# Moving the score mask, a softmax product and a value copy between engines in a recurrent-memory transformer kernel

## The chip, the cores and the metric

The kernel is one program on one core of a Trainium2 chip. It drives TensorE (PE, matrix products; PEld is its weight load), VectorE (DVE), ScalarE (ACT), GpSimd (POOL) and the DMA queue of SyncE (SP). The engines run side by side, each through its own list of instructions in order, and wait for each other on semaphores. The metric is the device time of one execution in microseconds (us), the median over several runs of the same program. Besides these runs one execution was recorded by the hardware profiler; all rows below come from it.

## The reference, cut to what matters

Two layers are applied to x (2048 rows of 512, bf16). The first one is attention that runs over segments of 32 rows and carries 8 rows of memory from one segment to the next:

```python
for s in range(64):
    h = concatenate([mem, x_norm[32 * s:32 * s + 32]])          # 40 rows of 512
    q, k, v = h @ Wq, h @ Wk, h @ Wv                            # 32 heads of 128
    scores = where(mask, q @ k.T * 128 ** -0.5, -1e9)           # 40 x 40 for each head
    o = (softmax(scores) @ v) @ Wo                              # 40 x 512
    mem, out[s] = o[:8], o[8:]
h = x + concatenate(out)
```

The second layer is a gated MLP with a mixing product over all 2048 rows (`h + ((z1 * (w_sp @ layernorm(z2) + b)) @ w_out)`, where z1 and z2 are halves of `gelu(layernorm(h) @ w_in)`). Because `mem` of a segment is an output of the segment before, the 64 segments are a chain.

## The kernel before, in words

**Order.** There is no scheduler. `Emitter` collects the instructions of each engine in the order in which the Python code names them, and adds semaphore waits wherever one reads or overwrites what another engine wrote (a token for each buffer, one token for each of the eight PSUM banks). Each engine runs its list strictly in that order. An instruction that has to wait for two engines gets a separate wait instruction in front of it.

**A segment.** The loop over `s` (lines 896 to 1025) names one segment after the other. In a segment heads are worked on in two halves, b = 0 and b = 1, of 16 heads. A "quarter" below is one of the four 128-deep slices of the 512-deep contraction: four matmuls of 32 columns of weights by 512 columns of data, one in each 32-column strip of the PE array, which run side by side. The order on PE is:

- `QK` (line 481): queries and keys of both halves, 64 matmuls. ACT copies each finished bank to `Tst` (line 488), and DVE transposes it in 32x32 blocks into `QT` (line 494) or `KT` (line 497). The first half of these products uses PSUM banks 0 (queries) and 1 (keys), the second half banks 6 and 7.
- `S_half(s, 0)`: scores of half 0 in bank 0. Four matmuls put the mask into the bank (line 511: identity times `mask`, 224 columns), then 16 + 4 small matmuls add the scores (lines 520 and 526). ACT takes the exponential into `E_sb` (`sm_exp`, line 534).
- `V_half(s, 0)`: values of half 0, four quarters into bank 6 (line 575); DVE copies them to `V_sb` (line 584).
- `sm_sums(0)`: products with ones that give the row sums (lines 541 and 546); ACT takes the logarithm (`sm_ln`, line 553) and then the reciprocal as an exponential (`sm_rcp`, line 557) into `R_sb`.
- `S_half(s, 1)` into bank 1, three quarters of `V_half(s, 1)` into bank 2, `sm_sums(1)`, and the last quarter of `V_half(s, 1)`. ACT copies bank 2 to `V_sb` (line 582).
- `sm_norm(0)` and `sm_norm(1)`, on DVE: two products each, `E_sb` times `R_sb` (line 561, 160 columns, and line 566, 64 columns). On POOL, `qx_copy(s + 1)` (line 504) puts the stored queries of the next segment into `QT`, once the scores of half 1 have been read.
- A **group** of work that does not depend on the recurrence, 16 matmuls: queries and keys of the memory-like x rows of a later chunk (`qkx_group`, line 411, segments 8 to 13 and 16 to 47), their values (`vx_group`, line 430, segments 0 to 7, 14 and 15), or a part of the second layer (`z2_group`, line 735, segments 49 to 63). Segment 48 has none.
- `PV_half(s, 0)` and `PV_half(s, 1)` (lines 592 and 598): probabilities times values, into banks 0, 1, 6 and 7. Half 1 needs `V_sb` of half 1 and the products of `sm_norm(1)`. ACT and DVE copy two banks each to `cT` (lines 611 and 613).
- `WoX_mm` (line 676, 8 matmuls, from segment 4 on), then one **atom** from `pour()`: a quarter of a further group (line 430 or 735). All segments have one but 45 to 48.
- `Wo` (line 625), the output product, which begins with the bank that ACT copied first. Then the 8 memory rows are put back to the front of the next segment (lines 649 and 654), and the next `QK` begins.

After the loop comes the second layer, whose lines the change does not touch.

**Lines that the change touches.** `S_half` (507 to 530), `sm_norm` (560 to 567), the constants `RBIAS`, `RK` and `UNSC`, and in the loop the lines 910 to 980.

Of the kernel before, what the change touches and what calls it, by code (L numbers as in the profile page):

```python
# [10 lines left out]
ALU = mybir.AluOpType  # L11
# [158 lines left out]
def fast_path(nc, st, keep, A_x, A_mem0, A_Wq, A_Wk, A_Wv, A_Wo, A_seg_len, B_w_in, B_w_sp, B_b_sp, B_w_out, out):  # L170
# [9 lines left out]
    DC = D // 128  # L180
# [10 lines left out]
    NEG = -1.0e30  # L191
    RBIAS = 44.42
    LNS = 2.0 ** -64
    RK = math.exp(-RBIAS)

    em = Emitter(n_dma_sems=40)
# [69 lines left out]
    def PB(b):  # L266
        return ("ps", b)
# [4 lines left out]
    def pe(fn, **k):  # L272
        return em.add("pe", fn, **k)
# [4 lines left out]
    def dve(fn, **k):  # L278
        return em.add("dve", fn, **k)
# [183 lines left out]
    SBK = (0, 1)  # L463
# [35 lines left out]
    def qx_copy(s):  # L499
# [5 lines left out]
             writes=[("QTe", 0), ("QTe", 1)])  # L505

    def S_half(s, b):
        bank = SBK[b]
        for c in range(4):
            q = slice(32 * c, 32 * c + 32)  # L510
            pe(lambda e, q=q, c=c: e.matmul(ps[q, bank, 0:224], lhsT=ident[:, q], rhs=mask[:, :], start=True, stop=False,  # L511
                                            skip_group_check=True, tile_position=(0, 32 * c)),
               reads=["ident", "mask"], writes=[PB(bank)])
        j = s % CK
# [44 lines left out]

    def sm_norm(b):  # L560
        dve(lambda e: e.scalar_tensor_tensor(out=E_sb[:, b, 0:160], in0=R_sb[:, b, :], scalar=RK, in1=E_sb[:, b, 0:160],  # L561
                                             op0=ALU.mult, op1=ALU.mult),
            reads=[("R", b), ("E", b)], writes=[("E", b)])
        ev = E_sb[:, b, 160:224].rearrange("p (g q) -> p g q", q=16)
        rv = R_sb[:, b, :].rearrange("p (g q) -> p g q", q=40)[:, :, 0:16]
        dve(lambda e: e.scalar_tensor_tensor(out=ev, in0=rv, scalar=RK, in1=ev, op0=ALU.mult, op1=ALU.mult),
            reads=[("R", b), ("Ex", b)], writes=[("Ex", b)])

# [34 lines left out]

    UNSC = 2.0 ** -64

# [143 lines left out]
    def z2_group():  # L749
        rb, hf = zx.pop(0)  # L750
        z2_narrow(rb, hf, XB)
        return lambda: z2_out(rb, hf, XB, "dve")
# [39 lines left out]
    def start_x(ck, i):  # L792
        start_group(qkx_mm, qkx_evac, ck, i)
# [102 lines left out]
    for s in range(NSEG):  # L896
# [17 lines left out]
        QK(s, 0, 0, (2, 3))  # L914
        QK_evac(s, 0, 0)
        QK(s, 0, 1, (2, 3))
        QK_evac(s, 0, 1)
        for mi in range(2):
            QK(s, 1, mi)
            lastop["qk"[mi]] = em.by_eng["pe"][-1]  # L920
            QK_evac(s, 1, mi)
        if s == 0:
            for n in range(2):
                start_v(n)
# [5 lines left out]
        V_half(s, 0)  # L930
        V_evac(0, "dve")
        sm_sums(0)
        sm_ln(0)
# [4 lines left out]
        if s == 0:  # L938
            for n in range(4, 8):
                start_v(n)  # L940
        V_half(s, 1, (0, 1, 2))
        sm_sums(1)
        sm_ln(1)
        sm_rcp(1)
        V_half(s, 1, (3,))
        lastop["v"] = em.by_eng["pe"][-1]
        if s == NSEG - 1:
            sp(lambda e: e.dma_start(w_in1, winr[:, :, 0:FH]), writes=["w_in1"], after=[lastop["s"], lastop["x"]])
            xn2T_dma(11, [lastop["s"], lastop["x"]])
            z2_back(0, 7, lastop["v"])  # L950
        V_evac(1, "act")
        sm_norm(0)
        sm_norm(1)
        if s + 1 < NSEG:
            qx_copy(s + 1)
            lastop["x"] = em.by_eng["pool"][-1]
            lastop["x"] = em.by_eng["pool"][-1]
        if s == 0:
            for j in range(2):
                load_vx(j, "pool")  # L960
            for i in range(8, 10):
                start_x(1, i)
        ev = [gx.pop(0)()] if gx else [z2_group()] if zx and s > 3 * CK else []
        PV_half(s, 0)
# [7 lines left out]
        if rb > 0:  # L972
            WoX_mm(rb - 1, j4)
            if j4 == 3:
                WoX_evac(rb - 1)
        late = pour()
        if j4 == 0 or (j4 == 2 and rb + 2 >= RB):
# [1021 lines left out]
```

## Time and profile before

| | |
|---|---|
| median of 3 runs | 879.51 us (879.2 to 880.05) |
| profiled execution, its own time | 879.29 us |
| span of its instructions | 877.6 us |
| granted TensorE clock | 0.997 |
| PE busy | 854.7 us (97%) |
| DVE busy | 487.4 us (56%) |
| ACT busy | 456.8 us (52%) |
| POOL busy | 110.8 us (13%) |

The span runs from the first instruction to the last; the execution's own time has 1.7 us more around it. The segments take from 38.5 us to about 713 us of the span, some 10.3 to 10.5 us each. A row of the timeline has the start in us, the duration in us, the engine, the line of the kernel, the operation, the buffers, the number of merged instructions, and in brackets how long the engine had been idle and what released it. A matmul's duration has its way through the array in it, so matmuls overlap, and the distance between starts says how long PE is taken. A row of a group has the busy time in us and the mean duration in ns behind the bar.

### The profile page before, as it was taken

The numbers are of one execution on the slowest core, as the hardware profiler recorded it, in microseconds if no ns is written. First come the engines' busy times: TensorE is split into PE (matmuls) and PEld (weight loads), VectorE is DVE, ScalarE is ACT, GpSimd is POOL, SyncE is SP. The second block draws the span as 40 slices with busy tenths as digits, with TensorE's granted clock in tenths as the row PEclk, the third lists the DMA queues.
The fourth block names the chain that finished last, engine by engine and source line by source line (L and its number), as shares of the span: only waits on it lengthen the run. The fifth ranks groups of instructions, "written<-read, shape, count | busy, mean of one in ns | idle before, by whom it ended". The sixth has DMA issues, their size and how long they took to land.

```text
span 877.6 us, 46595 instructions
## 1 busy us (share of the span) xinstructions
PE 854.7 (97%) x21446; PEld 487.1 (56%) x21453; DVE 487.4 (56%) x1128; ACT 456.8 (52%) x1147; POOL 110.8 (13%) x280
## 2 busy tenths in 40 slices
PE   6889999999999999999999999999999999999997
PEld 6645555555556666556566655555555544444443
DVE  2445566565556565555656565656555548363443
ACT  2346566666665666666666666566666566400000
POOL 1420111011111111110101010111111004100000
PEclk9999999999999999999999999999999999999999
DMA  9961222123321311212312121423322199122101
GB/s 322 377 191 44 75 52 67 37 61 59 63 55 38 72 52 31 72 34 64 61 31 64 46 61 37 111 68 88 69 68 62 55 214 352 32 102 83 57 13 38
DMA packets 109210, 76.35 MB, mean 87 GB/s; under 512 B 64104, under 2 KB 94512, under 8 KB 109008
## 3 DMA queue, kind: packets, MB, share of 16 engines
q1 hardware_dynamic: 108496, 73.04, 30.1%
q8 instruction: 170, 2.79, 1.3%
q14 instruction: 32, 0.26, 0.1%
q0 software_dynamic: 192, 0.20, 0.1%
q10 hardware_dynamic: 320, 0.07, 0.0%
HBM read 41.75 MB, written 20.91 MB: 71 GB/s over the span
## 4 chain that ended last, share of the span: by engine, by line
PE 94%; DVE 3%; DMA 1%; issue 1%; POOL 1%; ACT 0%; DVEq 0%
PE f_ps L481 26%; PE f_ps L625 13%; PE f_ps L575 12%; PE f_ps L1099 11%; PE f_ps L411 7%; PE f_ps L676 4%; PE f_ps L592 3%; PE f_ps L430 3%; PE f_ps L1193 3%; PE f_ps L1092 2%; PE f_ps L735 2%; PE f_ps L520 2%; PE f_ps L541 1%; PE f_ps L511 1%; DVE f_st L1074 1%; PE f_ps L649 1%
## 5 line engine op out<-in xcount | busy, mean ns | idle before, releaser
L481 PE MATMUL f_ps<-f_arena,f_hT 128*32 128x512 bf16 x4096 | 239.8, 380 | 0.2
L488 ACT ACTIVATE f_Tst<-f_ps 128x512 bf16<-128x512 f32 x256 | 145.9, 596 | 77.6 <-PE f_ps L481 77.4
L481 PEld LDWEIGHTS f_ps<-f_arena,f_hT 128*32 128x32 bf16 x4096 | 93.3, 96 | 103.0 <-ACT f_hT L654 32.4
L575 PE MATMUL f_ps<-f_arena,f_hT 128*32 128x512 bf16 x2048 | 140.4, 378 | 0.0
L625 PE MATMUL f_ps<-f_arena,f_cT 128*32 128x256 bf16 x4096 | 127.3, 272 | 0.8 <-ACT f_cT L611 0.8
L625 PEld LDWEIGHTS f_ps<-f_arena,f_cT 128*32 128x32 bf16 x4096 | 100.2, 96 | 20.6 <-ACT f_cT L611 18.8
L494 DVE STREAM_TRANSPOSE f_QT<-f_Tst 128x256 uint32<-128x256 uint32 x128 | 57.0, 446 | 90.2 <-ACT f_Tst L488 90.2
L1099 PE MATMUL f_ps<-f_arena 128*128 128x512 bf16 x448 | 99.6, 379 | 0.0
L613 DVE TENSOR_SCALAR f_cT<-f_ps 128x320 bf16<-128x320 f32 x128 | 56.9, 486 | 40.2 <-PE f_ps L598 40.2
L497 DVE STREAM_TRANSPOSE f_KT<-f_Tst 128x256 uint32<-128x256 uint32 x128 | 57.0, 445 | 29.2 <-ACT f_Tst L488 26.5
L1099 PEld LDWEIGHTS f_ps<-f_arena 128*128 128x128 bf16 x448 | 43.7, 98 | 52.6
L411 PE MATMUL f_ps<-f_hTe,f_arena 128*128 128x128 bf16 x1024 | 68.2, 225 | 4.2 <-DVE f_arena L422 3.1
L411 PEld LDWEIGHTS f_ps<-f_hTe,f_arena 128*128 128x128 bf16 x1024 | 60.6, 101 | 14.2 <-issue 9.4
L611 ACT ACTIVATE f_cT<-f_ps 128x320 bf16<-128x320 f32 x128 | 49.0, 435 | 37.3 <-PE f_ps L598 37.3
L504 POOL COPY f_QT<-f_arena 128x256 bf16<-128x256 bf16 x64 | 30.7, 479 | 296.8 <-PE f_ps L526 296.7
L561 DVE SCALAR_TENSOR_TENSOR f_E_sb<-f_R_sb,f_E_sb 128x160 bf16<-128x160 f32 x128 | 41.7, 326 | 46.3 <-ACT f_R_sb L557 46.3
L642 DVE CAST f_part<-f_ps 128x256 bf16<-128x256 f32 x64 | 27.2, 425 | 66.8 <-PE f_ps L625 66.8
L553 ACT ACTIVATE f_R_sb<-f_ps 128x160 f32<-128x160 f32 x128 | 38.8, 303 | 38.0 <-PE f_ps L546 38.0
L575 PEld LDWEIGHTS f_ps<-f_arena,f_hT 128*32 128x32 bf16 x2048 | 45.0, 95 | 21.2
L1105 DVE TENSOR_TENSOR f_arena<-f_ps,f_arena 128x512 f32<-128x512 f32 x28 | 19.3, 690 | 60.7 <-PE f_ps L1099 60.7
L654 ACT ACTIVATE f_hT<-f_ps 128x16 bf16<-128x16 f32 x126 | 23.1, 183 | 53.8 <-PE f_ps L649 53.3
L633 POOL COPY f_cTx<-f_cT 128x256 bf16<-128x256 bf16 x64 | 25.6, 401 | 196.3 <-DVE f_cT L613 196.3
(113 smaller groups left out, 1163.3 us busy)
## 6 DMA issues: line engine op xcount, KB each, us to landing
wT_d<-f_wst SPq DMA_DIRECT2D x32, 256.0 KB, 2.2
f_arena<-wT_d SPq DMA_DIRECT2D x32, 256.0 KB, 4.9
f_arena<-in_A_Wq_dram SPq DMA_DIRECT2D x4, 1024.0 KB, 8.9
f_arena<-in_A_Wk_dram SPq DMA_DIRECT2D x4, 1024.0 KB, 14.3
f_arena<-in_A_Wv_dram SPq DMA_DIRECT2D x4, 1024.0 KB, 14.5
f_arena<-in_A_Wo_dram SPq DMA_DIRECT2D x4, 1024.0 KB, 13.5
f_Vx<-vext_d SPq DMA_DIRECT2D x62, 64.0 KB, 2.9
vext_d<-f_Vs SPq DMA_DIRECT2D x24, 128.0 KB, 2.0
```

Source lines behind the costliest of these rows:

```text
L411: pe(lambda e, h=h, dc=dc, hh=hh: e.matmul(ps[:, bank, hh * 128:(hh + 1) * 128], lhsT=ws[:, dc, h * DH:(h + 1) * DH], rhs=hTe[:, ck % 3, d ...
L481: pe(lambda e, dc=dc, c=c, rhs=rhs: e.matmul(ps[32 * c:32 * c + 32, bank, :], lhsT=hT[:, sl, dc, :], rhs=rhs, start=(dc == 0), stop=(dc == ...
L488: act(lambda e: e.activation(out=Tst[:, tb, :].rearrange("p (hp i r) -> p hp i r", i=32, r=2), in_=ps[:, bank, :].rearrange("p (hp r i) -> ...
L494: dve(lambda e: e.transpose(out=dst, in_=src), reads=[("T", tb)], writes=[("QT", b)])
L497: dve(lambda e: e.transpose(out=dst, in_=src), reads=[("T", tb)], writes=[("KT", b)])
L553: act(lambda e: e.activation(out=R_sb[:, b, :], in_=ps[:, bank, 224:384], func=ACT.Ln, scale=LNS), reads=[PB(bank)], writes=[("R", b)])
L561: dve(lambda e: e.scalar_tensor_tensor(out=E_sb[:, b, 0:160], in0=R_sb[:, b, :], scalar=RK, in1=E_sb[:, b, 0:160], op0=ALU.mult, op1=ALU.m ...
L575: pe(lambda e, dc=dc, c=c, c0=c0: e.matmul(ps[32 * c:32 * c + 32, bank, :], lhsT=hT[:, sl, dc, :], rhs=w_v[:, dc, c0:c0 + 512], start=(dc ...
L611: act(lambda e: e.activation(out=dst, in_=src, func=ACT.Copy, scale=UNSC), reads=[PB(PVB[c])], writes=[("cT", c)])
L613: dve(lambda e: e.tensor_scalar(out=dst, in0=src, scalar1=UNSC, scalar2=None, op0=ALU.mult), reads=[PB(PVB[c])], writes=[("cT", c)])
L625: pe(lambda e, h=h, g=g, i=i, b=b, c=c: e.matmul(ps[32 * g:32 * g + 32, bank, 0:d1 - d0], lhsT=cTh[:, i, 8:40], rhs=w_o[:, h, d0:d1], star ...
L1099: pe(lambda e: e.matmul(ps[:, bank, 0:TB], lhsT=z2[:, sc, fb * 128:(fb + 1) * 128], rhs=wTb[tb % 2][:, :, sc, :], start=(n == 0), stop=(n ...
```

## The change

Five edits, all in the segment loop:

1. The eight mask matmuls of a segment (line 511) go. Instead DVE copies `mask` (128x224, bf16) into the score bank (float32 in PSUM), and the score matmuls add to what lies there. The copy for bank 0 stands on DVE's list behind the first transpose of half 0, ahead of its second one; the copy for bank 1 likewise in half 1.
2. `sm_norm(0)` goes from DVE to POOL, behind `qx_copy(s + 1)`. `sm_norm(1)` stays on DVE. Both become a plain product of two tensors; the constant factor goes into `RBIAS` and `UNSC`.
3. `V_evac(1)` goes from ACT to DVE, ahead of `sm_norm(1)`.
4. The first quarter of `V_half(s, 1)` goes ahead of `sm_sums(0)`; the other three stay ahead of `sm_sums(1)`, and none is left behind it (segment 0 does all four ahead of `sm_sums(1)`).
5. The first `pour()` of a segment, one atom, goes from between `WoX_mm` and `Wo` to ahead of the group, that is ahead of `PV_half`. What follows a finished atom (its copy and DMA) stays where it was.

```diff
-    RBIAS = 44.42
+    RBIAS = 34 * math.log(2.0)
     LNS = 2.0 ** -64
-    RK = math.exp(-RBIAS)
...
+    def mask_put(b):
+        bank = SBK[b]
+        dve(lambda e: e.tensor_copy(out=ps[:, bank, 0:224], in_=mask[:, :]), reads=["mask"], writes=[PB(bank)])
+
     def S_half(s, b):
         bank = SBK[b]
-        for c in range(4):
-            q = slice(32 * c, 32 * c + 32)
-            pe(lambda e, q=q, c=c: e.matmul(ps[q, bank, 0:224], lhsT=ident[:, q], rhs=mask[:, :], start=True, stop=False,
-                                            skip_group_check=True, tile_position=(0, 32 * c)),
-               reads=["ident", "mask"], writes=[PB(bank)])
...
-    def sm_norm(b):
-        dve(lambda e: e.scalar_tensor_tensor(out=E_sb[:, b, 0:160], in0=R_sb[:, b, :], scalar=RK, in1=E_sb[:, b, 0:160],
-                                             op0=ALU.mult, op1=ALU.mult),
-            reads=[("R", b), ("E", b)], writes=[("E", b)])
+    def sm_norm(b, on):
+        on(lambda e: e.tensor_tensor(out=E_sb[:, b, 0:160], in0=R_sb[:, b, :], in1=E_sb[:, b, 0:160], op=ALU.mult),
+           reads=[("R", b), ("E", b)], writes=[("E", b)])
         ev = E_sb[:, b, 160:224].rearrange("p (g q) -> p g q", q=16)
         rv = R_sb[:, b, :].rearrange("p (g q) -> p g q", q=40)[:, :, 0:16]
-        dve(lambda e: e.scalar_tensor_tensor(out=ev, in0=rv, scalar=RK, in1=ev, op0=ALU.mult, op1=ALU.mult),
-            reads=[("R", b), ("Ex", b)], writes=[("Ex", b)])
+        on(lambda e: e.tensor_tensor(out=ev, in0=rv, in1=ev, op=ALU.mult), reads=[("R", b), ("Ex", b)], writes=[("Ex", b)])
...
-    UNSC = 2.0 ** -64
+    UNSC = 2.0 ** -98
...
         QK_evac(s, 0, 0)
+        mask_put(0)
         QK(s, 0, 1, (2, 3))
...
             QK_evac(s, 1, mi)
+            if mi == 0:
+                mask_put(1)
...
         V_evac(0, "dve")
+        if s > 0:
+            V_half(s, 1, (0,))
         sm_sums(0)
...
-        V_half(s, 1, (0, 1, 2))
+        V_half(s, 1, (1, 2, 3) if s > 0 else range(DC))
+        lastop["v"] = em.by_eng["pe"][-1]
         sm_sums(1)
         sm_ln(1)
         sm_rcp(1)
-        V_half(s, 1, (3,))
-        lastop["v"] = em.by_eng["pe"][-1]
...
-        V_evac(1, "act")
-        sm_norm(0)
-        sm_norm(1)
         if s + 1 < NSEG:
             qx_copy(s + 1)
             lastop["x"] = em.by_eng["pool"][-1]
-            lastop["x"] = em.by_eng["pool"][-1]
+        sm_norm(0, pool)
+        V_evac(1, "dve")
+        sm_norm(1, dve)
...
+        late = pour()
         ev = [gx.pop(0)()] if gx else [z2_group()] if zx and s > 3 * CK else []
         PV_half(s, 0)
         PV_half(s, 1)
...
             if j4 == 3:
                 WoX_evac(rb - 1)
-        late = pour()
```

## The prediction

> **What bounds the kernel now.** I read the page first: busy shares and the chain that ended last.
>
> ```profile
> PE 854.7 (97%) x21446; PEld 487.1 (56%) x21453; DVE 487.4 (56%) x1128; ACT 456.8 (52%) x1147; POOL 110.8 (13%) x280
> PE 94%; DVE 3%; DMA 1%; issue 1%; POOL 1%; ACT 0%; DVEq 0%
> ```
>
> PE carries 94% of the chain, so what counts is each moment of PE in a segment. But matmul rows overlap, and "busy" hides short waits. So I went on to the timeline of one segment (number 31, in the middle) and read distances between starts. PE's rows:
>
> ```profile
> 372.06 0.61 PE L481 MATMUL f_ps<-f_arena,f_hT 128*32 128x512 bf16 x8
> ...
> 375.63 0.27 PE L511 MATMUL f_ps<-f_mask,f_ident 128*32 128x224 bf16 x4
> 375.73 0.27 PE L520 MATMUL f_ps<-f_QT,f_KT 128*32 128x40 bf16 x16
> ...
> 375.86 1.04 PE L575 MATMUL f_ps<-f_arena,f_hT 128*32 128x512 bf16 x16
> ...
> 376.87 0.27 PE L511 MATMUL f_ps<-f_mask,f_ident 128*32 128x224 bf16 x4
> 376.99 0.28 PE L520 MATMUL f_ps<-f_QT,f_KT 128*32 128x40 bf16 x16
> ...
> 377.79 0.25 PE L541 MATMUL f_ps<-f_E_sb,f_ones 128*32 128x160 bf16 x4
> ...
> 377.90 0.39 PE L575 MATMUL f_ps<-f_arena,f_hT 128*32 128x512 bf16 x4
> 378.22 1.07 PE L411 MATMUL f_ps<-f_hTe,f_arena 128*128 128x128 bf16 x16
> 379.22 0.27 PE L592 MATMUL f_ps<-f_E_sb,f_V_sb 32*128 32x40 bf16 x16
> 379.35 0.21 PE L598 MATMUL f_ps<-f_E_sb,f_Vx 32*128 32x64 bf16 x4
> 379.47 0.28 PE L592 MATMUL f_ps<-f_E_sb,f_V_sb 32*128 32x40 bf16 x16
> 379.57 0.21 PE L598 MATMUL f_ps<-f_E_sb,f_Vx 32*128 32x64 bf16 x4
> 379.71 0.61 PE L676 MATMUL f_ps<-f_arena,f_cTx 128*32 128x512 bf16 x8
> 380.15 0.39 PE L430 MATMUL f_ps<-f_arena,f_hTe 128*32 128x512 bf16 x4
> 380.37 1.70 PE L625 MATMUL f_ps<-f_arena,f_cT 128*32 128x256 bf16 x56
> ...
> 382.43 0.61 PE L481 MATMUL f_ps<-f_arena,f_hT 128*32 128x512 bf16 x8
> ```
>
> The segment takes 382.43 - 372.06 = 10.37 us. A mask costs PE 375.73 - 375.63 = 0.10 in half 0 and 376.99 - 376.87 = 0.12 in half 1; a quarter (the atom, 380.15 to 380.37) 0.22; a pair of sums 377.90 - 377.79 = 0.11. The other engines in the same segment:
>
> ```profile
> 374.33 0.45 DVE L494 STREAM_TRANSPOSE f_QT<-f_Tst 128x256 uint32<-128x256 uint32 x1 [1.86 <-ACT f_Tst L488]
> 375.62 0.45 DVE L494 STREAM_TRANSPOSE f_QT<-f_Tst 128x256 uint32<-128x256 uint32 x1 [0.36 <-ACT f_Tst L488]
> 376.49 0.45 DVE L497 STREAM_TRANSPOSE f_KT<-f_Tst 128x256 uint32<-128x256 uint32 x1 [0.42 <-ACT f_Tst L488]
> 377.10 0.30 ACT L553 ACTIVATE f_R_sb<-f_ps 128x160 f32<-128x160 f32 x1 [0.39 <-PE f_ps L546]
> 377.38 0.36 ACT L534 ACTIVATE f_E_sb<-f_ps 128x224 bf16<-128x224 f32 x1
> 377.41 0.48 POOL L504 COPY f_QT<-f_arena 128x256 bf16<-128x256 bf16 x1 [6.52 <-PE f_ps L526]
> 377.63 0.33 ACT L557 ACTIVATE f_R_sb<-f_R_sb 128x160 f32<-128x160 f32 x1
> 378.70 0.58 ACT L582 ACTIVATE f_V_sb<-f_ps 128x512 bf16<-128x512 f32 x1
> 378.83 0.33 DVE L561 SCALAR_TENSOR_TENSOR f_E_sb<-f_R_sb,f_E_sb 128x160 bf16<-128x160 f32 x1 [0.38 <-ACT f_R_sb L557]
> 379.07 0.22 DVE L566 SCALAR_TENSOR_TENSOR f_E_sb<-f_R_sb,f_E_sb 128x64 bf16<-128x64 f32 x1
> ```
>
> The reader should see three chains that run just behind PE. The last transpose ends at 376.49 + 0.45 = 376.94, and the scores of half 1 begin 0.05 later, at 376.99. ACT's value copy ends at 378.70 + 0.58 = 379.28 and DVE's products at 379.07 + 0.22 = 379.29, while PE is done issuing half 0 near 379.39 (half 1 takes 379.57 - 379.47 = 0.10 from its first to its x product, the last product some 0.04 more), but half 1 starts at 379.47. And from the last x product to `Wo` there are 380.37 - 379.57 = 0.80 us. How much of these is a wait, two other segments tell: number 45 has no atom, number 50 a shorter group.
>
> ```profile
> 525.00 0.21 PE L598 MATMUL f_ps<-f_E_sb,f_Vx 32*128 32x64 bf16 x4
> ...
> 525.74 0.51 PE L625 MATMUL f_ps<-f_arena,f_cT 128*32 128x256 bf16 x12
> ```
>
> ```profile
> 576.05 0.22 DVE L566 SCALAR_TENSOR_TENSOR f_E_sb<-f_R_sb,f_E_sb 128x64 bf16<-128x64 f32 x1
> ...
> 577.28 0.38 PE L625 MATMUL f_ps<-f_arena,f_cT 128*32 128x256 bf16 x5
> ```
>
> Without an atom `Wo` starts 525.74 - 525.00 = 0.74 after the last x product. That is the time the copy to `cT` needs. So the atom there, 0.22 of PE work, lengthens a segment by 0.80 - 0.74 = 0.06 alone.
>
> **The change part by part.**
>
> *Masks and the moved quarter (edits 1 and 4).* PE loses 0.22 a segment. With the quarter ahead of the first sums, the scores of half 1 could start at 375.63 + 0.13 (scores of half 0, 375.73 to 375.86) + 5 x 0.22 + 0.11 = 376.97. They need the last transpose, so they stay at 376.99. The gain appears behind the second sums: these stay at 377.79, and the quarter at 377.90 is gone.
>
> The copies must fit between DVE's transposes. No row shows DVE writing PSUM. The nearest are its reads from PSUM and its products:
>
> ```profile
> L642 DVE CAST f_part<-f_ps 128x256 bf16<-128x256 f32 x64 | 27.2, 425 | 66.8 <-PE f_ps L625 66.8
> L633 POOL COPY f_cTx<-f_cT 128x256 bf16<-128x256 bf16 x64 | 25.6, 401 | 196.3 <-DVE f_cT L613 196.3
> L362 POOL TENSOR_TENSOR f_rs<-f_rs,f_mhalf 128x1 f32<-128x1 f32 x20 | 11.3, 567 | 1.7
> L360 POOL TENSOR_SCALAR f_rs<-f_mv 128x1 f32<-128x1 f32 x20 | 4.5, 225 | 59.8 <-DVE f_mv L359 59.8
> ```
>
> 256 columns take 425 ns, 160 (line 561) 0.33 us, so 224 take about 0.39. Bounds: 0.22 (64 columns, line 566) and 0.58 (what ACT takes for 512, line 582). Half 1: first transpose to 375.62 + 0.45 = 376.07, copy to 376.46, and the second transpose starts at 376.49 anyway. Half 0: first transpose to 374.78, copy to 375.17, second to 375.62, where the scores want 375.63. Both fit by hundredths; I take 0.01 a segment, 0.6 us. DVE's independent products overlap by 0.09 (379.07 against 378.83 + 0.33), which may give slack.
>
> The first sums come 0.09 later (a quarter more, a mask less), so the first logarithm starts at 377.19. The exponential behind it, now at 377.38, could follow 0.2 later, as on ACT the next one starts 0.25 after one of 0.36 (377.38, 377.63). Cost nothing; if it had to wait for the logarithm's end, 377.49, 0.11.
>
> *First product on POOL (edit 2).* POOL is free at 377.41 + 0.48 = 377.89, the reciprocal at 377.63 + 0.33 = 377.96. Price of 160 and 64 columns: as a copy, 0.225 + (0.401 - 0.225) x 160/256 = 0.33 and 0.27; with 0.08 between them 0.68. From above, the one product of two tensors (a power, 0.567 for one column) plus the same slopes: 0.68 + 0.61 + 0.08 = 1.37. I take 0.85, nearer the copy, since a power is no plain product. It ends at 378.85 (378.7 to 379.4); PE wants it at 379.22 and 379.35. Hidden. PE's wait for two engines moves from half 1 to half 0, where PE also changes from x rows to the tiles of line 592; I cost it at nothing, at most 0.08.
>
> *Value copy on DVE (edit 3).* PE finishes it before the second sums, so DVE copies from about 378.0 to 378.7 (0.69 by the slope above), ahead of `sm_norm(1)` at 378.83. Half 1 then waits for one engine only. Its products end 379.16 and 379.29, and PE, which follows the last transpose by 0.05, is given 0.09 here with its weight load: 379.25 and 379.38. So half 1 starts at 379.39 instead of 379.47, its x product at 379.49.
>
> *Atom (edit 5).* It fills the 0.22 that the quarter left: group and `PV_half` start as before. `Wo` starts 0.74 after the x product: 379.49 + 0.74 = 380.23, not 380.37. Gain 0.14, with 0.16 of idle PE between line 676 (ends 380.15) and `Wo`, which the atom had covered.
>
> *Sum.* 35 segments (8 to 13, 16 to 44) have x rows and an atom: 35 x 0.14 = 4.9. In the other 28 (1 to 7, 14, 15, 45 to 63) PE reaches half 1 early and DVE's product decides. Segment 50: x product at 576.05 + 0.22 + 0.09 = 576.36, `Wo` at 577.10 instead of 577.28: 0.18, so 28 x 0.18 = 5.0. Together 9.9, less 0.6, is 9.3 us. The recorded execution took 879.29, 0.2 under the median: 879.29 - 9.3 = 870.0.
>
> **The rivals.** *Contention on the SBUF side.* In segment 0 POOL's copy and DVE's product met:
>
> ```profile
> 52.64 0.61 POOL L504 COPY f_QT<-f_arena 128x256 bf16<-128x256 bf16 x1
> 52.85 0.43 DVE L566 SCALAR_TENSOR_TENSOR f_E_sb<-f_R_sb,f_E_sb 128x64 bf16<-128x64 f32 x1
> ```
>
> Both were slow (0.48 and 0.22 elsewhere). DVE ended at 53.28, just behind POOL at 53.25. So if POOL is still at work at 378.83, `sm_norm(1)` is held: with POOL at its upper price it ends at 379.37, DVE loses 0.2 to 0.5, and each 0.1 costs 6.3 us. At a hold of 0.2, x rows gain 0.05 and the other segments lose 0.02: 879.3 - 1.2 = 878; at 0.35 it is slower, about 887. I say 878. The Trainium skill, page "SBUF — State Buffer", section "Who interferes with whom", states that a DVE instruction with two SBUF inputs contends with a GpSimd instruction that reads SBUF, and that the later one blocks until the first is done; the row agrees. [...]
>
> *The mask copy is too long* (the case of the other sign). It sits twice in DVE's chain to the last transpose. At c us a copy the scores of half 1 slip by 2c - 0.75 if DVE does not overlap, since 374.80 + c + 0.46 + 0.46 + c + 0.46 + 0.05 must be 376.99. The slip costs all 63 segments. It eats the gain of 9.3 at 0.15, so from c = 0.45; at 0.5 it is 0.25, 16 us lost, net 886; at the upper bound of 0.58, 0.41 and 896. For it: the copy writes PSUM, of which there is no price. Against it: copies of like size take 0.39 to 0.43.
>
> *The wait only moves.* PE's wait for two engines costs 0.08 at half 0 in the 35 segments with x rows: 873. With the exponential held by 0.05 more in all, 876.
>
> *The change shortens nothing but the gap before `Wo`*, if half 1 waits for something else: 35 x 0.06 = 2 us, 877.
>
> **How the numbers follow.** Forecast 0.56 (867 to 873, with the wait that moves inside it), contention or a slow POOL 0.14 (half of it slower, the rest same or faster), long mask copy 0.12 (two thirds slower), exponential held 0.09, gap alone 0.09 (half of it within the same). This kernel's measurement tells about 0.2%, 1.8 us, from no change. Faster: 0.56 + 0.09 + 0.045 + 0.035 + 0.02 = 0.75; same 0.10; slower 0.07 + 0.08 = 0.15. The predicted time is 870; the lower end, 866, is all of the masks' 14 us; the upper, 881, takes in contention and a slip a little past break-even, and leaves out the longest prices of both.
>
> **What would show it.** Right: no line 511; the last transpose still about 4.9 us into the segment; second sums at 5.73; half 1 of the probabilities about 0.14 behind the x product of half 0; 0.74 from the last x product to `Wo` with PE idle in it; segments of 10.22. Wrong: DVE's mask copies at 0.45 or more, POOL's products ending behind 378.9 with DVE's lengthened past 0.33, or the logarithm pushing the second exponential.

## The result and the profile after

The changed kernel takes 872.6 us (median; 870.0 to 873.3), the kernel before 879.6 us (879.0 to 881.8; its six runs include the three of the table above). The ratio is 0.9912, with a 95% interval of 0.9898 to 0.9927: 7 us, 0.9% faster. The recorded execution took 872.18 us, its span is 870.4 us. The page's line of busy time, and the first line of its chain that ended last (DVEq and POOLq are those engines' sequencers):

```profile
PE 846.9 (97%) x20941; PEld 474.5 (55%) x20941; DVE 527.5 (61%) x1192; ACT 420.9 (48%) x1083; POOL 161.6 (19%) x408
PE 95%; DVE 1%; DMA 1%; issue 1%; ACT 1%; POOL 1%; DVEq 0%; POOLq 0%
```

About 500 matmuls are gone from PE, DVE and POOL have taken work over, and PE's share of the chain is as large as before. Lines are numbered by the changed kernel from here on: 480 was 481, 518 was 520, 539 was 541, 571 was 575, 429 was 430, 410 was 411, 588 and 594 were 592 and 598, 672 was 676, 621 was 625, 487 was 488, 493 and 496 were 494 and 497, 503 was 504, 532 and 551 were 534 and 553; 508 is the new mask copy, 559 and 563 are the products of `sm_norm`, 580 is DVE's value copy. PE's rows of one segment with x rows (number 32, timeline):

```profile
377.61 0.61 PE L480 MATMUL f_ps<-f_arena,f_hT 128*32 128x512 bf16 x8
...
382.54 0.28 PE L518 MATMUL f_ps<-f_QT,f_KT 128*32 128x40 bf16 x16
...
383.33 0.25 PE L539 MATMUL f_ps<-f_E_sb,f_ones 128*32 128x160 bf16 x4
...
383.44 0.39 PE L429 MATMUL f_ps<-f_arena,f_hTe 128*32 128x512 bf16 x4
383.76 1.07 PE L410 MATMUL f_ps<-f_hTe,f_arena 128*128 128x128 bf16 x16
384.76 0.27 PE L588 MATMUL f_ps<-f_E_sb,f_V_sb 32*128 32x40 bf16 x16
384.89 0.21 PE L594 MATMUL f_ps<-f_E_sb,f_Vx 32*128 32x64 bf16 x4
384.92 0.28 PE L588 MATMUL f_ps<-f_E_sb,f_V_sb 32*128 32x40 bf16 x16
385.02 0.22 PE L594 MATMUL f_ps<-f_E_sb,f_Vx 32*128 32x64 bf16 x4
385.17 0.62 PE L672 MATMUL f_ps<-f_arena,f_cTx 128*32 128x512 bf16 x8
385.78 1.71 PE L621 MATMUL f_ps<-f_arena,f_cT 128*32 128x256 bf16 x56
...
387.85 0.40 PE L480 MATMUL f_ps<-f_arena,f_hT 128*32 128x512 bf16 x4
```

The segment takes 387.85 - 377.61 = 10.24 us, where it took 10.37. The scores of half 1 start 4.93 into it (382.54) and the second sums 5.72 (383.33), as before. The x product of half 0 is followed after 0.03 (384.89, 384.92) by half 1, where there were 0.12. From the last x product to `Wo` there are 0.76 us (385.02 to 385.78). The other engines in this segment:

```profile
380.25 0.37 DVE L508 CAST f_ps<-f_mask 128x224 f32<-128x224 bf16 x1
380.52 0.42 DVE L496 STREAM_TRANSPOSE f_KT<-f_Tst 128x256 uint32<-128x256 uint32 x1
...
381.40 0.60 ACT L487 ACTIVATE f_Tst<-f_ps 128x512 bf16<-128x512 f32 x1 [0.27 <-PE f_ps L480]
381.54 0.37 DVE L508 CAST f_ps<-f_mask 128x224 f32<-128x224 bf16 x1
382.03 0.45 DVE L496 STREAM_TRANSPOSE f_KT<-f_Tst 128x256 uint32<-128x256 uint32 x1
...
382.72 0.30 ACT L551 ACTIVATE f_R_sb<-f_ps 128x160 f32<-128x160 f32 x1 [0.47 <-PE f_ps L544]
382.92 0.36 ACT L532 ACTIVATE f_E_sb<-f_ps 128x224 bf16<-128x224 f32 x1
...
383.55 0.69 DVE L580 CAST f_V_sb<-f_ps 128x512 bf16<-128x512 f32 x1 [0.46 <-PE f_ps L571]
383.65 0.49 POOL L559 TENSOR_TENSOR f_E_sb<-f_R_sb,f_E_sb 128x160 bf16<-128x160 f32 x1 [0.22 <-ACT f_R_sb L555]
384.22 0.30 POOL L563 TENSOR_TENSOR f_E_sb<-f_R_sb,f_E_sb 128x64 bf16<-128x64 f32 x1
384.38 0.32 DVE L559 TENSOR_TENSOR f_E_sb<-f_R_sb,f_E_sb 128x160 bf16<-128x160 f32 x1
384.62 0.21 DVE L563 TENSOR_TENSOR f_E_sb<-f_R_sb,f_E_sb 128x64 bf16<-128x64 f32 x1
```

A mask copy takes 0.37, and the transpose behind it in half 0 starts 0.10 before the copy's end (380.25 + 0.37 against 380.52). In half 1 the mask copy is done at 381.91 and ACT's copy at 382.00; the last transpose starts at 382.03. POOL ends at 384.52, ahead of PE's start at 384.76. DVE's first product (384.38) begins while POOL is still in its second one and is not longer for it.

**Where the 7.2 us of span come from.** I took the distances between the first products of line 480 for segments 1 to 62, and for each kind of segment (1 to 3; 4 to 7, 14 and 15; those with x rows and atom; 45 to 47; 48 to 62) its usual length, the most frequent one to 0.01 us (for the two kinds of three, the shortest). The 35 with x rows have 10.24 (before 10.37), the other 27 have 10.09 to 10.10 (before 10.28 to 10.33). Summed, these steady lengths are 641.2 us before and 630.9 after: a steady gain of 10.3 us. But some segments are longer than usual. This excess, summed, is 1.5 us before and 5.7 after; it takes 4.2 back and leaves 6.1. The start is 0.5 us shorter, segment 0 and the rest of the program 0.3 each. The start varies by chance: it takes 38.0 and 38.7 us in the two recordings of the change, and 37.6 to 39.2 over those of all kernels.

Most of the excess is one segment. Number 48 takes 554.47 - 541.54 = 12.93 us, with 10.12 and 10.28 on either side of it and 10.29 before the change. PE's rows in it, from the timeline of the changed kernel:

```profile
549.55 0.39 PE L621 MATMUL f_ps<-f_arena,f_cT 128*32 128x256 bf16 x5
551.16 1.26 PE L621 MATMUL f_ps<-f_arena,f_cT 128*32 128x256 bf16 x20 [1.21 <-issue]
```

PE is idle for 1.21 us in the middle of `Wo`, and nothing that the profile shows released it. Then the clock falls. The windows of the same kernel (PE's busy time and its instructions first; the last three columns are the granted clock, the DMA share and GB/s; a packet counts in the window in which it starts, so the share can pass 1):

```profile
547.73:551.14 3.41, 1.71 (x53) 0.74 (x53) 1.79 (x5) 1.28 (x4) 1.04 (x3) 1.00 1.33 216
551.14:554.56 3.42, 3.40 (x71) 2.39 (x75) 0.00 (x0) 0.57 (x2) 0.00 (x0) 0.50 0.58 159
554.56:557.97 3.41, 3.39 (x71) 1.40 (x72) 2.24 (x6) 1.64 (x4) 0.79 (x2) 1.00 0.02 5
```

After a window in which PE was busy for 1.71 of 3.41 us, the clock was 0.5 for the next 3.41 us, and 1.00 again behind it.

### The profile page after: what moved, and what is told of

It reads as the page before. It is cut to its first block, busy times and chain, and to the rows that moved or that the text cites. A ratio compares the mean times of both kernels' runs of the same rounds, so it can differ in the third digit from the quotient of the medians.

```text
span 870.4 us, 45576 instructions
## 1 busy us (share of the span) xinstructions
PE 846.9 (97%) x20941; PEld 474.5 (55%) x20941; DVE 527.5 (61%) x1192; ACT 420.9 (48%) x1083; POOL 161.6 (19%) x408
## 3 DMA queue, kind: packets, MB, share of 16 engines
q8 instruction: 166, 2.72, 1.3%
## 4 chain that ended last, share of the span: by engine, by line
PE 95%; DVE 1%; DMA 1%; issue 1%; ACT 1%; POOL 1%; DVEq 0%; POOLq 0%
PE f_ps L480 26%; PE f_ps L621 15%; PE f_ps L571 12%; PE f_ps L1098 11%; PE f_ps L410 7%; PE f_ps L672 4%; PE f_ps L429 3%; PE f_ps L1091 3%; PE f_ps L1192 3%; PE f_ps L588 2%; PE f_ps L518 2%; PE f_ps L731 2%; PE f_ps L539 1%; PE f_ps L594 1%; PE f_ps L645 1%; PE f_ps L1059 1%
## 5 line engine op out<-in xcount | busy, mean ns | idle before, releaser
L480 PE MATMUL f_ps<-f_arena,f_hT 128*32 128x512 bf16 x4096 | 240.4, 380 | 0.1
L621 PE MATMUL f_ps<-f_arena,f_cT 128*32 128x256 bf16 x4096 | 130.8, 275 | 3.6 <-ACT f_cT L607 2.2
L571 PE MATMUL f_ps<-f_arena,f_hT 128*32 128x512 bf16 x2048 | 132.8, 378 | 0.0
L580 DVE CAST f_V_sb<-f_ps 128x512 bf16<-128x512 f32 x128 | 88.4, 691 | 29.5 <-PE f_ps L571 29.5
L636 ACT ACTIVATE f_part<-f_ps 128x256 bf16<-128x256 f32 x64 | 24.6, 384 | 46.5 <-PE f_ps L621 46.5
```

Of the source, the lines that this page charges most:

```text
L480: pe(lambda e, dc=dc, c=c, rhs=rhs: e.matmul(ps[32 * c:32 * c + 32, bank, :], lhsT=hT[:, sl, dc, :], rhs=rhs, start=(dc == 0), stop=(dc == ...
L571: pe(lambda e, dc=dc, c=c, c0=c0: e.matmul(ps[32 * c:32 * c + 32, bank, :], lhsT=hT[:, sl, dc, :], rhs=w_v[:, dc, c0:c0 + 512], start=(dc ...
L580: dve(lambda e: e.tensor_copy(out=V_sb[:, b, :], in_=ps[:, bank, :]), reads=[PB(bank)], writes=[("V", b)])
L621: pe(lambda e, h=h, g=g, i=i, b=b, c=c: e.matmul(ps[32 * g:32 * g + 32, bank, 0:d1 - d0], lhsT=cTh[:, i, 8:40], rhs=w_o[:, h, d0:d1], star ...
```

## The experiments

Theory A is the prediction's: a segment is as long as its gates make it, not as PE's work. The gates are the last transpose (scores of half 1), the end of DVE's or ACT's work for half 1 (second half of the probabilities), and 0.74 us from the last x product to `Wo`. Rival W: the time follows the work that PE loses. Further rivals stand with the runs. In the table the ratio is that to the kernel before, with its 95% interval; the last three columns, the usual length of segments with x rows, the steady sum of segments 1 to 62 and the excess, are from the recorded execution.

| kernel | median us | ratio | x rows | steady sum | excess |
|---|---|---|---|---|---|
| before | 879.3 to 880.4 | | 10.37 | 641.2 | 1.5 |
| the change | 872.6 | 0.9912 [0.9898, 0.9927] | 10.24 | 630.9 | 5.7 |
| the change, again | 873.9 | 0.9922 [0.9900, 0.9945] | 10.24 | 630.9 | 6.5 |
| e3, edits 1 and 4 alone | 879.4 | 0.9989 [0.9977, 1.0002] | 10.32 | 639.3 | 2.2 |
| e4, edits 2 and 3 alone | 880.9 | 1.0000 [0.9985, 1.0015] | 10.28 | 635.9 | 8.6 |
| e5, without edit 2 | 873.4 | 0.9935 [0.9921, 0.9950] | 10.24 | 634.1 | 2.6 |
| e6, without edit 3 | 876.8 | 0.9975 [0.9963, 0.9986] | 10.32 | 638.8 | 1.6 |
| e1, without edit 5 | 870.8 | 0.9882 [0.9859, 0.9906] | 10.15 | 628.4 | 4.7 |
| e2, atom by kind | 870.6 | 0.9889 [0.9869, 0.9910] | 10.14 | 627.2 | 4.4 |
| e2, again | 868.1 | 0.9871 [0.9855, 0.9887] | 10.14 | 627.2 | 3.7 |
| e7, mask copies twice | 890.1 | 1.0119 [1.0105, 1.0134] | 10.53 | 649.0 | 4.5 |
| e8, POOL late | 880.7 | 1.0013 [1.0004, 1.0021] | 10.32 | 640.0 | 2.7 |
| e9, more DMA traffic | 876.9 | 0.9962 [0.9946, 0.9977] | 10.24 | 630.9 | 6.4 |
| e10, one load moved | 868.1 | 0.9868 [0.9847, 0.9889] | 10.14 | 627.2 | 3.3 |

### Masks and quarter alone (e3), products and value copy alone (e4)

e3 keeps edits 1 and 4 of the change and undoes the rest:

```diff
+        V_evac(1, "act")
+        sm_norm(0, dve)
+        sm_norm(1, dve)
         if s + 1 < NSEG:
             qx_copy(s + 1)
             lastop["x"] = em.by_eng["pool"][-1]
-        sm_norm(0, pool)
-        V_evac(1, "dve")
-        sm_norm(1, dve)
...
-        late = pour()
         ev = [gx.pop(0)()] if gx else [z2_group()] if zx and s > 3 * CK else []
...
+        late = pour()
         if j4 == 0 or (j4 == 2 and rb + 2 >= RB):
```

> Edits 1 and 4 alone: masks by DVE copies, the quarter ahead of the first sums; both softmax products on DVE, the second value copy on ACT, the atom behind line 676. PE loses 0.22 us of work a segment, 14 us in all. Theory A (gate): ACT's value copy still ends at +7.22 and holds the second half of the probabilities at about +7.37 (before: +7.41 with x rows, +7.37 without), so Wo gains at most 0.04 in 35 segments and nothing in 28: 1 to 2 us, about 878. Rival W (the time follows the work taken from PE, and the 7.0 us of the whole change are half of these 14): 872 to 874 here already.

It gives 1 us, with an interval that reaches to nothing. From its timeline, in a segment with x rows (its line 578 is ACT's value copy):

```profile
386.80 0.58 ACT L578 ACTIVATE f_V_sb<-f_ps 128x512 bf16<-128x512 f32 x1
```

```profile
387.10 0.27 PE L588 MATMUL f_ps<-f_E_sb,f_V_sb 32*128 32x40 bf16 x16
387.22 0.21 PE L594 MATMUL f_ps<-f_E_sb,f_Vx 32*128 32x64 bf16 x4
387.52 0.28 PE L588 MATMUL f_ps<-f_E_sb,f_V_sb 32*128 32x40 bf16 x16
```

Half 0 starts 0.22 earlier in the segment than before the change (6.94 instead of 7.16), as the masks' work is gone. PE then stands still until ACT's copy ends at 387.38 and starts half 1 at 387.52. Of 14 us of PE work taken away, 1 us is seen. This speaks for A and against W, which asks for 872 to 874 here.

e4 does the opposite: masks by matmul, the quarter and the atom where they were, and of the change only these lines, with the new form of `sm_norm` and its constants (shown against the kernel before):

```diff
-        V_evac(1, "act")
-        sm_norm(0)
-        sm_norm(1)
...
+        sm_norm(0, pool)
+        V_evac(1, "dve")
+        sm_norm(1, dve)
```

> Edits 2 and 3 alone: first softmax product on POOL, second value copy on DVE; masks by matmul, the quarter behind the second sums and the atom behind line 676 as before. PE has all its old work. Theory A (gate): the value copy starts 0.25 later than in the change (the quarter ends later), 6.2 to 6.9, DVE's second product 6.9 to 7.36; with x rows the second half of the probabilities starts at +7.30 instead of +7.41 and Wo at +8.20 instead of +8.31, 35 x 0.11 = 3.9 us; elsewhere at +7.28 instead of +7.37, 28 x 0.05 = 1.4 us: 5 us faster than before, 874.5. Rival W (time follows PE's work): no PE work is taken, 879.6.

The steady segments do what A says: 10.28 with x rows (0.09 less, expected 0.11) and 0.08 to 0.09 less in most others (expected 0.05); the steady sum is 5.3 us lower. But the time is that of the kernel before: the recorded excess is 8.6 instead of 1.5 us and takes it all back. PE's waits for issue in e4, two rows of its list of waits over the whole span (total in us, times, longest):

```profile
PE f_ps L677 <- issue: 1.6, 1, 1.6
...
PE f_ps L375 <- issue: 0.7, 1, 0.7
```

The first lies in segment 48, which takes 13.14 us and has half the clock in a part of it, as in the change. In the kernel before the list has a single wait of PE for issue:

```profile
PE f_ps L430 <- issue: 0.2, 1, 0.2
```

So W names the right time for e4, for a reason that it doesn't have, and A has the steady part right and nothing about these stalls. In time, each of these halves alone is worth 0 to 1 us; edits 1 to 4 together (e1 below) are worth 9.6.

### The first product back on DVE (e5), the value copy back on ACT (e6)

e5 is the change with one word replaced:

```diff
-        sm_norm(0, pool)
+        sm_norm(0, dve)
```

> The change with its edit 2 undone: the first softmax product on DVE again, ahead of the second value copy, which stays on DVE. Theory A (the gate is the end of DVE's chain): from the end of the reciprocal at +5.90, DVE does the first product to about +6.40, the copy from +6.32 to +7.01 and the second product to +7.26 and +7.40, so the second half of the probabilities starts at about +7.32 and ends its x product at +7.46, against +7.16 and +7.29 without x rows and +7.31 and +7.41 with them: 28 x 0.17 + 35 x 0.04 = 6 us slower than the change, 879. Rival S (DVE has time for both, the move to POOL is worth nothing): 872.6. Rival N (DVE's four operations cannot overlap: 0.3 later): 885 or more.

With x rows nothing is lost (10.24, expected 0.04 more), in the others 0.12 (expected 0.17). In one of those (it starts at 584.67) the first product of `sm_norm(1)` starts 6.91 into it, in the change 6.77. The price is no higher since DVE's operations overlap by 0.08 or so:

```profile
590.98 0.69 DVE L580 CAST f_V_sb<-f_ps 128x512 bf16<-128x512 f32 x1
591.58 0.32 DVE L559 TENSOR_TENSOR f_E_sb<-f_R_sb,f_E_sb 128x160 bf16<-128x160 f32 x1
```

The steady sum is 3.2 us above the change's, and the excess 3.1 us lower, so the time is nearly the same, and the two intervals overlap. The move to POOL is worth at most those 3.2 us, and nothing in segments with x rows.

e6 undoes edit 3:

```diff
-        V_evac(1, "dve")
+        V_evac(1, "act")
```

> The change with its edit 3 undone: the second value copy on ACT again, behind the second reciprocal. Theory A (ACT's copy ends at +7.22 as before the change, and PE, which then waits for ACT and for DVE, starts the second half at +7.37): Wo 0.18 later in 28 segments and 0.08 later in 35, 5 + 2.8 = 8 us slower than the change, 880.5. Rival O (no price on the second wait; PE starts 0.06 behind ACT): 28 x 0.09 = 2.5 us slower, 875. Rival S (the value copy on DVE is worth nothing): 872.6.

The steady segments are as A has it to the hundredth: 0.08 longer with x rows, 0.18 in the others. The median of 876.8 is under the 880.5 expected, as the excess is 1.6 and not the change's 5.7. Two rows of a segment without x rows, ACT's copy and DVE's first product, and what PE made of them:

```profile
593.19 0.58 ACT L578 ACTIVATE f_V_sb<-f_ps 128x512 bf16<-128x512 f32 x1
```

```profile
593.31 0.33 DVE L559 TENSOR_TENSOR f_E_sb<-f_R_sb,f_E_sb 128x160 bf16<-128x160 f32 x1 [1.29 <-ACT f_R_sb L555]
```

```profile
593.91 0.28 PE L588 MATMUL f_ps<-f_E_sb,f_V_sb 32*128 32x40 bf16 x16
```

ACT ends at 593.77 and PE starts 0.14 later. In the change it waits for DVE alone and starts 0.06 behind it (product 6.77 to 7.10 into the segment, PE at 7.16). So the second wait costs about 0.08; that is the term of which rival O says it is nothing. A slower signal from ACT is not the reason: where PE waits for ACT alone, at the second sums, it starts 0.05 behind the exponential's end (the median in e6, in the change and before it).

### The atom (e1, e2)

e1 puts `late = pour()` back behind line 672. e2 does so only in the segments with x rows:

```diff
-        late = pour()
+        xrow = 8 <= s < 14 or 16 <= s < 45
+        late = [] if xrow else pour()
...
                 WoX_evac(rb - 1)
+        if xrow:
+            late = pour()
```

> The change without its edit 5: the atom (pour) stands behind line 676's products again, ahead of Wo. Theory A (Wo starts 0.74 to 0.76 us behind the last x product, and the second half of the probabilities starts when DVE's products are done): in segments with x rows the idle 0.17 us ahead of Wo is filled with the atom, the x rows come 0.32 earlier, the second half of the probabilities then waits for DVE's product and starts at +7.16 instead of +7.31, Wo at about +8.09 instead of +8.17: 35 x 0.08 = 2.8 us gained; in the other segments the atom now comes late and Wo starts at +8.09 instead of +8.03: 28 x 0.05 = 1.4 us lost. Net 1.4 us faster than the change, 871. Theory B (the order of the atom does not matter, PE has the same work): as the change, 872.6. Theory C (edit 5 carries the gain before Wo, as before the change): slower by the 0.06 that the atom cost there, 63 x 0.06 = 4 us, 876.

> The change with the atom behind line 676's products only in segments 8 to 13 and 16 to 44 (those with x rows), ahead of the group elsewhere. Theory A: 35 x 0.08 = 2.8 us faster than the change, 869.8; segments with x rows 10.16 instead of 10.24, the others unchanged at 10.09 to 10.11. Theory B (order of the atom does not matter): 872.6. Theory C: 35 x 0.06 slower, 874.7.

> The change with the atom behind line 676's products in the segments with x rows, again, now beside the change itself. Theory A (Wo follows the last x product by 0.75, and the idle time ahead of it is free for the atom): segments with x rows 10.14 instead of 10.24, 35 x 0.10 = 3.5 us faster than the change, 868.5. Rival (what the steady segments gain is lost in irregular ones): 870 to 872.

Edit 5 costs time where there are x rows. PE's rows of e2 in such a segment:

```profile
391.74 0.21 PE L594 MATMUL f_ps<-f_E_sb,f_Vx 32*128 32x64 bf16 x4
391.83 0.27 PE L588 MATMUL f_ps<-f_E_sb,f_V_sb 32*128 32x40 bf16 x16
391.96 0.21 PE L594 MATMUL f_ps<-f_E_sb,f_Vx 32*128 32x64 bf16 x4
392.10 0.62 PE L672 MATMUL f_ps<-f_arena,f_cTx 128*32 128x512 bf16 x8
392.54 0.39 PE L429 MATMUL f_ps<-f_arena,f_hTe 128*32 128x512 bf16 x4
392.76 1.70 PE L621 MATMUL f_ps<-f_arena,f_cT 128*32 128x256 bf16 x56
```

Half 1 now waits a little for DVE (0.09 behind the x product of half 0), the atom covers the time until `Wo`, and `Wo` starts 8.09 into the segment instead of 8.17. The segments go from 10.24 to 10.14, 35 x 0.10 = 3.5 us. In e1 most of the others lose 0.03 to 0.04, as the atom comes late there. Beside the change, e2 takes 868.1 against 873.9: the two intervals, 0.9855 to 0.9887 and 0.9900 to 0.9945, don't meet. In the first runs, which were not beside each other, they overlapped (0.9869 to 0.9910 and 0.9898 to 0.9927), with medians of 870.6 and 872.6. **e2 beats both kernels**, by 0.2 to 0.5% the change and by 1.1 to 1.3% the kernel before. The two later recordings differ by 6.0 us of span: 3.7 in the steady sums, 2.8 in the excess (3.7 and 6.5), 0.9 in the start and segment 0, less 1.4 that e2 loses behind segment 62: there PE waits 1.3 us for the transfer of the spatial weights (`wT_d`, line 1101 of e2), for which it doesn't wait in the change. Theories B and C fall.

### The rivals of the prediction: a longer mask (e7), a later POOL (e8)

e7 makes each mask copy twice:

```diff
-        dve(lambda e: e.tensor_copy(out=ps[:, bank, 0:224], in_=mask[:, :]), reads=["mask"], writes=[PB(bank)])
+        for _ in range(2):
+            dve(lambda e: e.tensor_copy(out=ps[:, bank, 0:224], in_=mask[:, :]), reads=["mask"], writes=[PB(bank)])
```

> The change with each of DVE's mask copies made twice. By the prediction's formula (slip 2c - 0.75, no overlap on DVE; c = 0.37 + 0.37 - 0.08): 0.57 a segment, 36 us slower, 908. By the overlap that the trace of the change shows (each operation starts 0.07 to 0.1 ahead of the end of the one before; ACT's copy, not the mask, holds the last transpose): the second mask adds about 0.29 to a chain with 0.14 to 0.18 of room in half 0 and 0.09 to 0.22 in half 1, so scores move by about 0.11: 7 us slower, 879.5. If the mask copies hung on nothing: 872.6.

18 us slower than the change (the steady sums differ by 18.1), between the two numbers expected. DVE's rows in one segment (the two copies are one row):

```profile
380.11 0.80 DVE L509 CAST f_ps<-f_mask 128x224 f32<-128x224 bf16 x2
380.82 0.43 DVE L496 STREAM_TRANSPOSE f_KT<-f_Tst 128x256 uint32<-128x256 uint32 x1
381.18 0.40 DVE L493 STREAM_TRANSPOSE f_QT<-f_Tst 128x256 uint32<-128x256 uint32 x1
381.50 0.80 DVE L509 CAST f_ps<-f_mask 128x224 f32<-128x224 bf16 x2
382.21 0.43 DVE L496 STREAM_TRANSPOSE f_KT<-f_Tst 128x256 uint32<-128x256 uint32 x1
```

The two copies don't overlap (0.80 for both), since the program makes the second wait for the first: `Emitter` adds a wait also between two instructions of DVE that write the same bank. Each of the other four operations starts 0.07 to 0.09 before the end of the one ahead. A further copy thus adds 0.43, not the 0.29 that I expected. DVE has no idle time left from the first transpose to the last, and the scores of half 1 start 5.22 into the segment instead of 4.93: 0.29 later, which reaches its end. The prediction's slip, 2c - 0.75, would have given 2 x 0.80 - 0.75 = 0.85 with the 0.80 that both copies take. It leaves out the overlaps at five handovers, 0.07 to 0.09 each and 0.42 in all, and it takes 0.13 too much for the four transposes (0.45, 0.43, 0.40 and 0.43): 0.30, near the 0.29 seen. The rival is real, but by these overlaps its point of no gain lies further out than I put it.

e8 makes POOL's copy of line 503 twice, so that POOL's products come later:

```diff
-            qx_copy(s + 1)
+            for _ in range(2):
+                qx_copy(s + 1)
```

> The change with POOL's copy of line 503 made twice, so that POOL's two products run about 0.42 later, at +6.46 to +6.95 and +7.03 to +7.33, and both lie beside DVE's second products (+6.77 to +7.10, +7.02 to +7.23). Without contention (theory A): DVE's products keep 0.33 and 0.21 us and their places; PE's x product of half 0 waits for POOL to +7.38 and half 1 follows: 0.10 later in 35 segments, 0.23 in 28: 10 us slower than the change, 882.5. With contention on the SBUF side (rival): DVE's products end with POOL's, at +6.95 + 0.33 or later and +7.55: 0.2 and 0.32 later, 16 us slower, 888.5, and their mean rises above 0.4 and 0.3.

The change would take 871.6 to 872.5 beside these runs (its two ratios times 879.3), so e8 is 8 to 9 us slower: near the 10 us of A, not the 16 of contention. The rows of DVE and of POOL in one segment:

```profile
366.68 0.33 DVE L559 TENSOR_TENSOR f_E_sb<-f_R_sb,f_E_sb 128x160 bf16<-128x160 f32 x1
366.93 0.36 DVE L563 TENSOR_TENSOR f_E_sb<-f_R_sb,f_E_sb 128x64 bf16<-128x64 f32 x1
```

```profile
366.34 0.49 POOL L559 TENSOR_TENSOR f_E_sb<-f_R_sb,f_E_sb 128x160 bf16<-128x160 f32 x1
366.90 0.31 POOL L563 TENSOR_TENSOR f_E_sb<-f_R_sb,f_E_sb 128x64 bf16<-128x64 f32 x1
```

DVE's long product ran beside POOL's and kept its 0.33. Its short one took 0.36 instead of 0.21 and ended at 367.29, 0.08 behind POOL's (367.21). It is so over the whole span: the means of 64 are 333 and 358 ns, against 329 and 218 in the change. So there is contention, as in segment 0 before the change, but it held DVE by 0.15 in one of the two overlaps, and in the change itself in none. The Trainium skill's page "SBUF — State Buffer", section "Who interferes with whom", would have the later instruction wait for the earlier one to end. The short product agrees with it; the long one, which began while POOL's had 0.15 to go and was not longer, goes against it. POOL's recorded spans are rough, so how long POOL really held SBUF is not known.

### What makes segments irregular (e9, e10)

In the long segment 48, 896 KB of second-layer weights, two transposing loads and others fill the DMA engines. The DMA rows of the changed kernel for 545.4 to 548.4, the 3 us before the stall:

```profile
q1 hardware_dynamic: 883, 0.96, 95.2%
q8 instruction: 1, 0.02, 2.9%
```

The program comes as pieces of 16 KB through the same engines. That queue q8 is PE's is inferred from its size, 2.72 of the 2.99 MB of instructions on the page. By its packets one comes each 4.3 us on average between 60 and 700 us of the span; the longest interval is 7.0 us and ends with the piece at 548.4, in front of this stall. In e1, e2 and the second recording of the change the longest (7.4 to 8.0) lies in the same place; before the change it is 6.1. Theory I: PE's instructions come late. e9 tries it with more traffic (the first diff, against the change); e10 is e2 with a part of the burst moved (the second, without the lines of e2):

```diff
-        if s % 2 == 1 and s // 2 < NWT:
+        if s >= 1 and s // 2 < NWT:
             wT_piece(s // 2)
```

```diff
-        if s % 2 == 1 and s // 2 < NWT:
+        if s % 2 == 1 and s // 2 < NWT and s != 49:
             wT_piece(s // 2)
+        if s == 50:
+            wT_piece(24)
```

> The changed kernel once more, beside the three that follow. All theories: about 872. What is looked at: whether segment 48 is long again (12.9 us in the first profile, 10.1 for its neighbours), with TensorE idle about 1.2 us for nothing that the profile shows.

> The change with the transposing load and the store of one 64-row piece of the spatial weights issued in every segment instead of every second one, so that each piece is written twice with the same values: twice that DMA traffic, and nothing that TensorE computes hangs on it. Theory I (the irregular stalls are instructions that arrive late, since their packets pass through the same busy DMA engines): more segments are lengthened by 0.1 to 1 us at TensorE waits that the profile puts down to issue, the steady ones stay at 10.24 and 10.09; the excess over the steady length, 5.5 us in the first profile of the change, rises to 9 or more: 876 or more. Rival J (the stalls have to do with TensorE alone): 872. Rival D (data arrives late): longer too, but with TensorE waiting for named DMA transfers.

> The kernel of e2_again with one transposing load, the piece of the spatial weights of segment 49, issued one segment later, at the start of segment 50. In the first profiles it is issued on SP's queue in the middle of segment 48, behind the 896 KB of the second input weights and two transposing loads, and TensorE's long stall (1.2 to 1.5 us) follows within 1 to 3 us. Theory I (late instructions, because of that burst): segment 48 goes from about 11.9 to 10.1 to 10.6, 1.3 to 1.8 us faster than e2_again. Rival (the input weights' load or the two transposing loads ahead of it do it, or the stall has another cause): segment 48 stays at 11.5 to 12.9.

The change again had its long segment 48 (12.59 us, 0.88 of it idle for issue). e9 is slower than the change beside it by 3 us, and the intervals don't meet; the median of 876.9 is as theory I has it. But its recorded execution, 1.7 us under that median, has an excess of 6.4 against 6.5 and not 9, with 1.2 us more in segment 0 (22.8 for 21.6). So e9 neither bears theory I out nor refutes it. e10 leaves segment 48 at 11.51, just where it is in e2's second recording, and the instructions' piece is as late (7.6 us). So the load that I moved is not the cause. The weights' load and the two transposing loads ahead of it remain; I have not tried them. That late instructions cause the stall is argued from their place in time, not shown.

What the runs do show is with which edit the stall goes. All eleven recordings of kernels with the second value copy on DVE (edit 3) have an idle time of PE for issue in segment 48, of 0.8 to 1.6 us, and the segment takes 11.5 to 13.1 us. The three without it (the kernel before, e3 and e6) have none, and the segment takes 10.3. The longest interval between q8's pieces is 6.8 to 8.0 us in the eleven and 6.1 to 6.5 in the three. Shorter segments are not the condition: in segments with x rows e6 and e8 both take 10.32, and only e8 has the stall (0.91). The executions that were not recorded agree. One window at half the clock lowers the mean granted clock by about 0.002 (half of 3.41 in 872 us); it is 0.996 or less in 50 of the 77 executions with edit 3, in 2 of the 20 of e3 and e6, and in 9 of the 58 of the kernel before that were run beside the experiments. How the engine of the value copy brings the stall about stays open.

## Why the prediction was right, point by point

The forecast of 870 had the change's mechanism, with its size a little low in the steady segments, and lacked a loss. In the recorded executions the 9.3 us that it counts came out as 7.2 of span: 1.0 more in the steady segments, 4.2 lost to excess, and 1.1 gained in the start, segment 0 and the rest, which the sum doesn't have. That it lies within 3 us of the result is in part luck.

- **Masks and quarter.** As predicted, the scores of half 1 and the second sums stay at +4.93 and +5.73. The copies take 0.37 (0.39 taken). The 0.01 a segment that I charged for them isn't there: in half 1 ACT's copy sets the last transpose (382.00, 382.03), not the mask (381.91). The formula of the rival, 2c - 0.75, would have charged 0.03 at the 0.39 taken. That the exponential follows the logarithm by 0.2 is borne out (382.72, 382.92).
- **POOL.** 0.49 + 0.08 + 0.30 = 0.87 us (0.85 taken), ending 0.24 before PE needs it. It starts 0.14 behind the reciprocal's end (383.51, 383.65), where the sum has 0.04 (its 378.85 - 0.85 against 377.96).
- **Value copy and single wait.** Half 1 follows half 0 directly in segments with x rows. The 0.14 that the prediction names as a sign is the distance of the two x products (here 0.13, from 384.89 to 385.02); half 1 itself starts 0.03 behind the x product of half 0, where its sum has 379.39 - 379.35 = 0.04. e6 confirms the gate and the 0.08 for a second wait. That this price did not move to half 0 is seen too: half 0 starts at +7.15, as before.
- **`Wo`.** With x rows it starts at +8.17, as predicted; the segment comes out at 10.24 and not 10.22, as 0.01 are lost behind it and the prediction's own 10.37 - 0.14 is 10.23. In the others `Wo` gains 0.22 and not 0.18. The mis-sized terms are PE's start behind DVE's last product, 0.06 for the 0.09 taken, and the way from the last x product to `Wo`, 0.72 or 0.73 there for 0.74. The steady sum is 10.3 us for 9.9 - 0.6 = 9.3.
- **Edit 5.** I counted the atom as filling the quarter's place and noted 0.16 us of idle PE in front of `Wo`. The same rows said that the atom could have filled this gap, and that edit 5 is a loss of 0.1 in 35 segments; I didn't draw that. e2 did.
- **What failed:** the sum took every segment for a steady one. 4.2 us of 10.3 went into longer excess, above all into segment 48 with its issue stall and its half clock (12.93 - 10.09 = 2.8). Before the change all excess was 1.5 us, and no row of it gave this size. As the stall goes with edit 3, the value copy's move is worth some 4 to 5 us in the time (e6: 876.8 against 872.6, or the ratios 0.9975 against 0.9912 and 0.9922) and not the 7.9 of its steady segments. The loss differs from execution to execution: of the change's twelve, the two with a granted clock of 0.998 took 869.8 and 870.0 us, the two with 0.993 took 875.0 and 875.2.
- **The rivals.** Of 0.43 us more for each mask copy 0.29 reach the end of the segment (e7), so a somewhat longer copy would have been hidden; where between 0.37 and 0.80 the loss begins was not measured. Contention exists (e8), but not at this POOL's time. The gap alone would have gained 0.06 in segments with x rows, where 0.13 were seen, and nothing in the others.

## What to carry to other kernels

Work taken from the busiest engine shows only up to the next gate: here 14 us of matmuls were worth 1 us until the wait behind them was moved as well (e3), and moving the wait alone gained 5.3 us in the steady segments and nothing in the time (e4). When a wait has gone, look again at what used to fill it: the independent atom belonged in front of `Wo` in one kind of segment and ahead of the group in the other. And compare the median segment with the mean one, since a shorter steady segment can be paid back in a few long ones.

## What the runs showed of the hardware

- **A clock gate in the middle of a run.** After a stall the clock was 0.5 for one window of 3.41 us. The change (twice), e1, e4, e7 and e9 have it begin in segment 48, which then takes 12.6 to 13.1 us; e2 (twice), e5, e8 and e10 have a stall of the same kind without it, and take 11.5 to 11.9. e1, e7 and e9 have such a window in segment 0 too, and there take 22.8 to 23.4 us where the other kernels take 21.1 to 21.9. PE's busy time in the window ahead doesn't separate them: 1.6 to 2.2 of 3.4 us with it, 1.9 to 2.3 in the windows of e2 and e10 that hold the stall. The Trainium skill, page "TensorE: Matmul & The Clock Gate", Part 1, states windows of 3413 ns and the half rate after at least one idle window; length and rate agree, but here the clock fell behind a window in which PE was busy for 1.71 us, with the gap of 1.21 us and a part of the one of 0.58 (548.13) in it.
- **DVE overlaps operations that don't depend on each other** by 0.07 to 0.10 us, copies into PSUM and transposes too (the change and e7).
- **A wait for a second engine** costs PE some 0.08 us (e6: 0.14 behind the later one instead of 0.06; behind ACT alone it is 0.05).
